# Reordering a filter's reversed copies in the SyncE queue, and moving the end of the last output slab from GpSimd to VectorE

One core of a Trainium2 chip. The metric is the device time of one execution in microseconds (us), median of several executions; "span" is the same from first to last instruction in the profiled execution.

## The reference

A layer norm, a spectral filter on one side, a gated feed-forward on the other, and a product:

```python
xn = _layernorm(x)                                    # x: 1 x 2048 x 640, bf16
s  = irfft2(rfft2(xn) * (w_r + 1j * w_i))             # filter w: 2048 x 321
g  = silu((gelu(xn @ w_gate) * (xn @ w_up)) @ w_down) # 640 -> 1536 -> 640
out = x + s * g
```

## The kernel before

The kernel is a list of tasks (instruction, engine, estimated cost, rank, predecessors), from which a planner in Python makes a fixed order for each engine ahead of time. It issues, at each step, the ready task with the lowest rank; a cost that is too low makes it believe that an engine (or the SyncE queue) is free early. The two Fourier transforms are matmuls and run interleaved with the feed-forward, so that TensorE is never out of work.

The filter is applied in eight groups G of rows. Each group needs its filter rows twice: as they are, and reversed. The reversal is done by DMA alone: a copy from DRAM to a DRAM scratch `D4` with a negative step (line 609, called "copy" below), and a load of the scratch into SBUF (line 632, "read-back"). Cut to that:

```python
for ri, w in enumerate((A_w_r, A_w_i)):
    for G in range(8):
        turned_w[G].append(add(lambda e, ...: nc.sync.dma_start(            # line 609: the reversing copy
            out=D4[:, b:8 * G + 8, ri, :], in_=bass.AP(..., ap=[[P * L, NSLAB], [-L, 8 * G + 8 - b], [1, LP]])),
            "SP", (430, 430), (2, G), after=[turned[3]] if G < 2 else [B_in[3]], ...))
...
def fetch(G):
    sw = Slot("W")                                     # three buffers WF in turn
    ...
    t = add(lambda e: go(e, 0, A_w_r), "SP", (430, 430), (3, G), after=hold, ...)   # line 625: rows as they are
    t = add(lambda e: go(e, 1, A_w_i), "SP", (430, 430), (3, G), after=hold, order=[t], ...)
    ...
    W_in[G] = add(back, "SP", (430, 430), (3, G), after=hold + turned_w[G], order=[t], ...)  # line 632: read-back
```

VectorE multiplies filter and spectrum (lines 738 and 746), forms `Y` (742, 749) and from it `R` (759, 761), which is what TensorE takes for the inverse transform (line 781, with the table TI as weights). TI is one more load in the same queue.

The last output slab (128 x 640) is finished in three parts of 256, 256 and 128 columns. The feed-forward's result lies in PSUM (`ps`), `th` is its tanh by ScalarE, `y` the filter's result, `sx` the input rows:

```python
def f1(e): (nc.gpsimd if last and lo == 0 else nc.vector).tensor_tensor(out=yg, in0=y, in1=G2, op=mult)   # line 954
def f2(e): (nc.gpsimd if last and lo == 0 else nc.vector).tensor_tensor(out=res, in0=yg, in1=sx, op=add)  # line 959
...
for lo, hi, tag in parts:
    ...
    a = add(tanh, "ACT", ...)                          # line 981
    if last and lo:                                    # parts 2 and 3
        t = add(early, "DVE", ...)                     # line 992: mc = y * ps    (f32)
        t = add(late, "DVE", ...)                      # line 995: yg = (th + 1) * mc
        t = add(... res = yg + sx ..., "DVE", ...)     # line 1001
        ... store part 2 by SyncE's queue, part 3 by ScalarE's (line 1004)
        continue
    done.append(add(silu, "DVE", ...))                 # line 986: G2 = (th + 1) * ps
    finish(lo, hi, ...)                                # lines 954, 959, store by SyncE's queue
```

Of the kernel before, what the change touches and what calls it, by code (L numbers as in the profile page):

```python
# [14 lines left out]
ALU = mybir.AluOpType  # L15
P = 128
S = 2048
D = 640
# [198 lines left out]
def c_dve(n, rate=2, psum=False, extra=0):  # L217
    d = ((120 if psum else 58) + n / rate) / 0.96 + extra
    return d + 10, d + 130
# [3 lines left out]
def kernel(  # L223
# [11 lines left out]
    nc = tc.nc  # L235
# [51 lines left out]
    add = plan.add  # L287
# [91 lines left out]
    t = add(blank, "DVE", (330, 400), (0, -9), new=[idle])  # L379
    t = warmed = keep_warm(6, [t])  # L380
# [225 lines left out]
    for ri, w in enumerate((A_w_r, A_w_i)):  # L606
        for G in range(8):
            b = 8 * G if G else 2
            turned_w[G].append(add(lambda e, ri=ri, w=w, G=G, b=b: nc.sync.dma_start(  # L609
                out=D4[:, b:8 * G + 8, ri, :], in_=bass.AP(tensor=w.tensor, offset=w.offset + (P - b) * L, ap=[[P * L, NSLAB], [-L, 8 * G + 8 - b], [1, LP]])),  # L610
                                   "SP", (430, 430), (2, G), after=[turned[3]] if G < 2 else [B_in[3]], size=82432, slow=1.7))
        for a, n, b, first, width in ((0, 8, 0, 1088, LP), (8, 7, 0, 1152, LP), (15, 1, 0, 1024, LP), (0, 15, 1, P - 1, LP), (15, 1, 1, S - 1, L)):
            turned_w[0].append(add(lambda e, ri=ri, w=w, a=a, n=n, b=b, first=first, width=width: nc.gpsimd.dma_start(
                out=D4[a:a + n, b, ri, 0:width], in_=rows(w, first, n, width)), "POOL", (600, 600), (9, ri, b, a), after=[roots[15]], size=5152))
        turned_w[0].append(add(lambda e, ri=ri, w=w: nc.gpsimd.dma_start(out=D4[15:16, 1, ri, L:LP], in_=w[0:1, 0:1]), "POOL", (600, 600),
                            (9, ri, 2), after=[roots[15]], size=64))

    def fetch(G):
        sw = Slot("W")
        W_slot[G] = sw  # L620

        def go(e, ri, w):
            sw.tile = WF[G % 3]
            c = 1 if G == 0 else 0
            nc.sync.dma_start(out=sw.tile[16 * c:P, 0, ri, 0:L], in_=w.rearrange("(k c) f -> c k f", c=P)[8 * G + c:8 * G + 8])

        def zero(e, ri, w):
            nc.sync.dma_start(out=sw.tile[0:16, 0, ri, 0:L],
                              in_=bass.AP(tensor=w.tensor, offset=w.offset, ap=[[64 * L, 2], [P * L, 8], [1, L]]))

        def back(e):
            nc.sync.dma_start(out=sw.tile[:, 1].rearrange("p r f -> p (r f)"), in_=D4[::-1, 8 * G:8 * G + 8].rearrange("a c r f -> c a (r f)"))
        hold = [stored[7]] + ([B_in[2 * G - 2]] if 0 < G < 3 else [])
        t = add(lambda e: go(e, 0, A_w_r), "SP", (430, 430), (3, G), after=hold, order=[W_in[G - 1]] if G else [], new=[sw], size=82176, slow=1.2)
        t = add(lambda e: go(e, 1, A_w_i), "SP", (430, 430), (3, G), after=hold, order=[t], use=[sw], size=82176, slow=1.2)
        if G == 0:
            for ri, w in enumerate((A_w_r, A_w_i)):
                t = add(lambda e, ri=ri, w=w: zero(e, ri, w), "SP", (430, 430), (3, G), after=hold, order=[t], use=[sw], size=10272, slow=1.2)
        W_in[G] = add(back, "SP", (430, 430), (3, G), after=hold + turned_w[G], order=[t], use=[sw], size=164352, slow=1.2)

    for G in range(8):
        fetch(G)
# [295 lines left out]
    def down(n1):  # L938
# [11 lines left out]
        def finish(lo, hi, done, rank, first):  # L950
            def f1(e):
                if first:
                    place(yg, (D,))
                (nc.gpsimd if last and lo == 0 else nc.vector).tensor_tensor(out=yg.tile[:, lo:hi], in0=y.tile[:, n1 % 2, lo:hi], in1=G2.tile[:, lo:hi], op=ALU.mult)

            def f2(e):
                if first:
                    place(res, (D,))
                (nc.gpsimd if last and lo == 0 else nc.vector).tensor_tensor(out=res.tile[:, lo:hi], in0=yg.tile[:, lo:hi], in1=sx.tile[:, lo:hi], op=ALU.add)  # L959
            slow = last and lo == 0  # L960
            t = add(f1, *(("POOL", (700, 800)) if slow else ("DVE", c_dve(hi - lo))), rank, after=[y_done[n1]] + done, new=[yg] if first else [], use=[y, G2] if first else [y, G2, yg])
            t = add(f2, *(("POOL", (700, 800)) if slow else ("DVE", c_dve(hi - lo))), rank, after=[t, xr], new=[res] if first else [], use=[yg, sx] if first else [yg, sx, res])
            dma(lambda: outv[:, n1, lo:hi], lambda: res.tile[:, lo:hi], (0, 0, n1), 256 * (hi - lo), after=[t], use=[res])

        for lo, hi, tag in parts:
            ps, th, mm = Slot(tag), Slot("th"), []
            for k in range(0, 12, 6):
                def go(e, k=k, lo=lo, hi=hi, ps=ps):
                    if k == 0:
                        place(ps, (512,))  # L970
                    for i in range(k, k + 6):
                        nc.tensor.matmul(ps.tile[:, 0:hi - lo], lhsT=uT[grp, ks[i]].tile[:, j * P:(j + 1) * P], rhs=Wd[:, ks[i], lo:hi],  # L972
                                         start=(i == 0), stop=(i == 11))
                step[0] += 1
                mm.append(add(go, "PE", c_pe(*[hi - lo] * 6), (1, step[0]), new=[] if k else [ps],
                              after=[u_done[grp, t] for t in ks[k:k + 6]] + mm + [d_in[t] for t in ks[k:k + 6]],
                              use=[uT[grp, t] for t in ks[k:k + 6]] + ([ps] if k else [])))

            def tanh(e, lo=lo, hi=hi, ps=ps, th=th):
                place(th, (320,), FP32)  # L980
                nc.scalar.activation(out=th.tile[:, 0:hi - lo], in_=ps.tile[:, 0:hi - lo], func=ACT.Tanh, scale=0.5)  # L981

            def silu(e, lo=lo, hi=hi, ps=ps, th=th):
                if lo == 0:
                    place(G2, (D,))
                nc.vector.scalar_tensor_tensor(out=G2.tile[:, lo:hi], in0=th.tile[:, 0:hi - lo], scalar=1.0, in1=ps.tile[:, 0:hi - lo],  # L986
                                               op0=ALU.add, op1=ALU.mult)
            yp = Slot("mc")

            def early(e, lo=lo, hi=hi, ps=ps, yp=yp):  # L990
                place(yp, (hi - lo,), FP32)
                nc.vector.tensor_tensor(out=yp.tile, in0=y.tile[:, n1 % 2, lo:hi], in1=ps.tile[:, 0:hi - lo], op=ALU.mult)

            def late(e, lo=lo, hi=hi, th=th, yp=yp):
                nc.vector.scalar_tensor_tensor(out=yg.tile[:, lo:hi], in0=th.tile[:, 0:hi - lo], scalar=1.0, in1=yp.tile,
                                               op0=ALU.add, op1=ALU.mult)
            a = add(tanh, "ACT", c_act(hi - lo), (0, step[0]), after=mm[-1:], new=[th], use=[ps])
            if last and lo:
                t = add(early, "DVE", c_dve(hi - lo, 1, True), (0, step[0]), after=mm[-1:] + [y_done[n1]], new=[yp], use=[ps, y])
                t = add(late, "DVE", c_dve(hi - lo, 1), (0, step[0]), after=[a, t] + done, use=[th, yp, yg])  # L1000
                t = add(lambda e, lo=lo, hi=hi: nc.vector.tensor_tensor(out=res.tile[:, lo:hi], in0=yg.tile[:, lo:hi], in1=sx.tile[:, lo:hi], op=ALU.add),
                        "DVE", c_dve(hi - lo), (0, step[0]), after=[t, xr], use=[yg, sx, res])
                if hi == D:
                    add(lambda e, lo=lo: nc.scalar.dma_start(out=outv[:, n1, lo:], in_=res.tile[:, lo:]), "ACT", (430, 430), (0, 0, n1),
                        after=[t], use=[res], size=256 * (hi - lo))
                else:
                    dma(lambda lo=lo, hi=hi: outv[:, n1, lo:hi], lambda lo=lo, hi=hi: res.tile[:, lo:hi], (0, 0, n1), 256 * (hi - lo), after=[t], use=[res])
                continue
            done.append(add(silu, "DVE", c_dve(hi - lo, 1, True), (0, step[0]), after=[a] + done, new=[] if lo else [G2],
                            use=[ps, th, G2] if lo else [ps, th]))  # L1010
            if last:
                finish(lo, hi, [done[-1]], (0, step[0]), lo == 0)
# [42 lines left out]
```

## Time and profile before

| | before |
|---|---|
| time, first three runs | 205.31 us (205.14 to 205.66) |
| profiled execution: time, span | 205.79 us, 204.0 us |
| TensorE busy | 195.1 us (96%) |
| last matmul ends; last store issued; span ends | 199.27; 201.03; 204.0 |

TensorE sets the pace: what matters is where it is *not* busy. The prediction shows the lines for it. One more line, from the timeline of SyncE's queue of the kernel before, tells how such lines are to be read (start, duration, engine, line, output and input):

```profile
85.17 0.63 SPq L632 DMA_DIRECT2D WF<-D  x1
```

The 0.63 us is the time that the queue spends on issuing. The Trainium skill, "Perfetto Trace Analysis", section "Per-instruction lifecycle: what the profiler-reported window actually captures", says that the window of such a DMA instruction holds the making of its descriptors and not the movement of data. This trace agrees: the same DMA landed 4.15 us after its issue, by the chain of waits.

### The profile page before, as it was taken

Reading aid. Unit: us, or ns where it says so; the run is one execution under the profiler, and the core shown is the slowest. Engines: PE = TensorE matmul, PEld = TensorE weight load, DVE = VectorE, ACT = ScalarE, POOL = GpSimd, SP = SyncE. Lnnn points to the kernel's source line nnn. Section 1 sums busy time; section 2 is a strip of 40 time slices with the busy share of each in tenths; the row PEclk is TensorE's granted clock in tenths of the full one; section 3 lists DMA queues with packets and bytes.
Section 4 is the critical chain, followed back from the end, with each engine's and each line's share of the span. In section 5 each row is a group of like instructions: output and inputs, shape, how many; then the busy total and the mean of one; then the engine's idle time right before and its main releaser. Section 6 shows DMA issues by size and latency. Waiting matters only on the chain.

```text
span 204.0 us, 4147 instructions
## 1 busy us (share of the span) xinstructions
PE 195.1 (96%) x1530; PEld 117.9 (58%) x1547; DVE 147.4 (72%) x312; ACT 129.1 (63%) x230; POOL 33.4 (16%) x72
## 2 busy tenths in 40 slices
PE   7999999999999999979999999999999999999990
PEld 2894444676444555756754555467765555557780
DVE  3589879999233259949999999943257789888763
ACT  4999699964822777666766776333467666675420
POOL 2413233799000000000000000000001122210211
PEclk9999999999999999999999999999999999999998
DMA  6999999698977957653243301116701243332421
GB/s 177 328 314 329 342 391 200 144 157 216 160 268 253 310 165 184 115 169 120 69 130 91 105 21 47 64 39 221 322 0 47 87 130 110 110 101 67 132 98 64
DMA packets 35894, 32.62 MB, mean 160 GB/s; under 512 B 10910, under 2 KB 32930, under 8 KB 35874
## 3 DMA queue, kind: packets, MB, share of 16 engines
q1 hardware_dynamic: 34434, 29.49, 49.5%
q0 software_dynamic: 1152, 2.66, 5.8%
q10 hardware_dynamic: 288, 0.20, 0.5%
q8 instruction: 12, 0.20, 0.4%
q14 instruction: 8, 0.07, 0.1%
HBM read 22.51 MB, written 9.19 MB: 155 GB/s over the span
## 4 chain that ended last, share of the span: by engine, by line
PE 74%; DMA 14%; SPq 4%; DVE 3%; issue 1%; ACT 1%; DVEq 0%
PE pu L894 20%; PE pg L894 19%; PE pu L972 11%; PE pg L972 11%; DMA BU<-D 5%; SPq L609 3%; DMA D<-mc 3%; PE sp L839 3%; DMA WF<-in_A_w_r_dram 2%; PE sp L815 2%; DMA WF<-D 2%; PE sp L781 2%; DMA X<-in_A_x_dram 2%; PE sp L541 2%; PE sp L706 1%
## 5 line engine op out<-in xcount | busy, mean ns | idle before, releaser
L894 PE MATMUL pu<-xnT,Wu 128*128 128x512 bf16 (+1 forms) x237 | 56.7, 365 | 0.5
L894 PE MATMUL pg<-xnT,Wg 128*128 128x512 bf16 (+1 forms) x236 | 56.3, 365 | 0.4
L911 DVE TENSOR_TENSOR uT<-pu,ge 128x512 bf16<-128x512 f32 x46 | 31.7, 689 | 21.2 <-PE pu L894 17.7
L972 PEld LDWEIGHTS <-uT 128*128 128x128 bf16 x396 | 37.9, 98 | 13.5
L907 ACT ACTIVATE ge<-pg 128x512 bf16<-128x512 f32 x46 | 27.5, 598 | 24.4 <-PE pg L894 23.5
L894 PEld LDWEIGHTS <-Wg 128*128 128x128 bf16 x285 | 25.1, 98 | 22.5 <-issue 0.3
L894 PEld LDWEIGHTS <-Wu 128*128 128x128 bf16 x285 | 25.0, 98 | 21.8
L935 POOL DMA_DIRECT2D xr<-in_A_x_dram x16 | 8.8, 550 | 135.8 <-DVE res L959 135.8
L972 PE MATMUL pg<-Wd,uT 128*128 128x320 bf16 (+2 forms) x204 | 30.7, 293 | 0.0
L297 ACT CAST ma<-sp 128x644 bf16<-128x644 f32 (+1 forms) x32 | 23.4, 793 | 9.7 <-PE sp L839 7.9
L972 PE MATMUL pu<-Wd,uT 128*128 128x320 bf16 (+1 forms) x192 | 29.5, 297 | 0.0
L297 ACT CAST IU<-sp 128x640 bf16<-128x640 f32 x16 | 10.9, 691 | 5.1 <-PE sp L781 5.1
L981 ACT ACTIVATE th<-pu 128x320 f32<-128x320 f32 (+1 forms) x16 | 7.0, 435 | 10.7 <-PE pu L972 10.1
L981 ACT ACTIVATE th<-pg 128x320 f32<-128x320 f32 (+2 forms) x17 | 7.3, 429 | 10.0 <-PE pg L972 8.5
L297 ACT CAST Vt<-sp 128x640 bf16<-128x640 f32 x16 | 10.8, 691 | 3.7 <-PE sp L815 3.7
L986 DVE SCALAR_TENSOR_TENSOR G<-th,pg 128x320 bf16<-128x320 f32 (+1 forms) x16 | 7.7, 479 | 6.9 <-ACT th L981 6.9
L297 ACT CAST mc<-sp 128x640 bf16<-128x640 f32 x16 | 10.7, 704 | 1.3 <-PE sp L542 1.3
L986 DVE SCALAR_TENSOR_TENSOR G<-th,pu 128x320 bf16<-128x320 f32 x15 | 7.3, 484 | 5.3 <-ACT th L981 5.1
L434 POOL TENSOR_TENSOR RSTD<-MVA,mh 128x1 f32<-128x1 f32 x12 | 8.9, 743 | 6.6 <-DVE MVA L416 5.9
L419 ACT ACTIVATE th<-X 128x640 bf16<-128x640 bf16 x11 | 8.1, 739 | 1.7 <-DMA D<-th 1.6
L857 DVE TENSOR_TENSOR mb<-ma 128x640 bf16<-128x640 bf16 x8 | 3.9, 493 | 7.0 <-ACT ma L297 7.0
L738 DVE TENSOR_TENSOR mc<-WF,mb 128x1288 bf16<-128x1288 bf16 x8 | 6.6, 826 | 3.1 <-DMA WF<-D 3.0
(110 smaller groups left out, 248.5 us busy)
## 6 DMA issues: line engine op xcount, KB each, us to landing
BU<-D SPq DMA_DIRECT2D x8, 640.0 KB
D<-mc SPq DMA_DIRECT2D x8, 320.0 KB
xr<-in_A_x_dram POOLq DMA_DIRECT2D x16, 160.0 KB, 2.6
D<-IU SPq DMA_DIRECT2D x8, 320.0 KB
out_dram<-res SPq DMA_DIRECT2D x15, 160.0 KB
Wg<-in_B_w_gate_dram SPq DMA_DIRECT2D x6, 320.0 KB
Wu<-in_B_w_up_dram SPq DMA_DIRECT2D x6, 320.0 KB
Wd<-in_B_w_down_dram SPq DMA_DIRECT2D x6, 320.0 KB
```

What stands on the lines that cost most here:

```text
L297: return nc.scalar.copy(out=out, in_=in_) if e == "ACT" else nc.vector.tensor_copy(out=out, in_=in_)
L419: nc.scalar.activation(out=place(junk, (D,)), in_=x, func=ACT.Copy, scale=-1.0 / D, accum_out=less)
L434: nc.gpsimd.tensor_tensor(out=rstd, in0=var, in1=mh, op=ALU.pow)
L609: turned_w[G].append(add(lambda e, ri=ri, w=w, G=G, b=b: nc.sync.dma_start(out=D4[:, b:8 * G + 8, ri, :], in_=bass.AP(tensor=w.tensor, off ...
L738: nc.vector.tensor_tensor(out=sM.tile, in0=sw.tile, in1=sV.tile, op=ALU.mult)
L894: nc.tensor.matmul(ps.tile[:, lo:hi], lhsT=w[:, c, t * P:(t + 1) * P], rhs=XR[:, c, lo:hi] if early else xnT[:, c, grp * 512 + lo:grp * 51 ...
L907: nc.scalar.activation(out=ge.tile, in_=pg.tile if src is None else src, func=ACT.Gelu_apprx_tanh)
L911: nc.vector.tensor_tensor(out=u.tile, in0=pu.tile if src is None else src, in1=ge.tile, op=ALU.mult)
L935: nc.gpsimd.dma_start(out=sx.tile, in_=xv[:, n1, :])
L972: nc.tensor.matmul(ps.tile[:, 0:hi - lo], lhsT=uT[grp, ks[i]].tile[:, j * P:(j + 1) * P], rhs=Wd[:, ks[i], lo:hi], start=(i == 0), stop=(i ...
L981: nc.scalar.activation(out=th.tile[:, 0:hi - lo], in_=ps.tile[:, 0:hi - lo], func=ACT.Tanh, scale=0.5)
L986: nc.vector.scalar_tensor_tensor(out=G2.tile[:, lo:hi], in0=th.tile[:, 0:hi - lo], scalar=1.0, in1=ps.tile[:, 0:hi - lo], op0=ALU.add, op1 ...
```

## The change

Intent: a reversing copy of group G should be issued just ahead of the loads of the group in front of it, instead of all copies together ahead of group 2's read-back; the planner's cost of an issue is put nearer to the trace's 0.64 us; and GpSimd is taken off the end, its part and the middle part both going through lines 986, 954 and 959 on VectorE.

```diff
-   "SP", (430, 430), (2, G), after=[turned[3]] if G < 2 else [B_in[3]], ...            # copies, line 609
+   "SP", (650, 650), (2, G) if G < 2 else (3, G - 1.5), after=[turned[3]] if G < 2 else [B_in[3]], ...
 ...
-   t = add(lambda e: go(e, 0, A_w_r), "SP", (430, 430), (3, G), ...                    # loads and read-back
+   t = add(lambda e: go(e, 0, A_w_r), "SP", (680, 680), (3, G), ...                    # (all four lines alike)
 ...
-   (nc.gpsimd if last and lo == 0 else nc.vector).tensor_tensor(out=yg..., op=ALU.mult)
+   (nc.gpsimd if n1 in () else nc.vector).tensor_tensor(out=yg..., op=ALU.mult)        # never GpSimd; f2 alike
 ...
-   if last and lo:
+   if last and hi == D:                                                                # only part 3 by 992, 995
```

More of the change, by code (lines that the diff above doesn't have):

```diff
@@ L610 @@
                 out=D4[:, b:8 * G + 8, ri, :], in_=bass.AP(tensor=w.tensor, offset=w.offset + (P - b) * L, ap=[[P * L, NSLAB], [-L, 8 * G + 8 - b], [1, LP]])),
-                                   "SP", (430, 430), (2, G), after=[turned[3]] if G < 2 else [B_in[3]], size=82432, slow=1.7))
+                                   "SP", (650, 650), (2, G) if G < 2 else (3, G - 1.5), after=[turned[3]] if G < 2 else [B_in[3]], size=82432, slow=1.7))
         for a, n, b, first, width in ((0, 8, 0, 1088, LP), (8, 7, 0, 1152, LP), (15, 1, 0, 1024, LP), (0, 15, 1, P - 1, LP), (15, 1, 1, S - 1, L)):
@@ L633, in fetch @@
         hold = [stored[7]] + ([B_in[2 * G - 2]] if 0 < G < 3 else [])
-        t = add(lambda e: go(e, 0, A_w_r), "SP", (430, 430), (3, G), after=hold, order=[W_in[G - 1]] if G else [], new=[sw], size=82176, slow=1.2)
-        t = add(lambda e: go(e, 1, A_w_i), "SP", (430, 430), (3, G), after=hold, order=[t], use=[sw], size=82176, slow=1.2)
+        t = add(lambda e: go(e, 0, A_w_r), "SP", (680, 680), (3, G), after=hold, order=[W_in[G - 1]] if G else [], new=[sw], size=82176, slow=1.2)
+        t = add(lambda e: go(e, 1, A_w_i), "SP", (680, 680), (3, G), after=hold, order=[t], use=[sw], size=82176, slow=1.2)
         if G == 0:
             for ri, w in enumerate((A_w_r, A_w_i)):
-                t = add(lambda e, ri=ri, w=w: zero(e, ri, w), "SP", (430, 430), (3, G), after=hold, order=[t], use=[sw], size=10272, slow=1.2)
-        W_in[G] = add(back, "SP", (430, 430), (3, G), after=hold + turned_w[G], order=[t], use=[sw], size=164352, slow=1.2)
+                t = add(lambda e, ri=ri, w=w: zero(e, ri, w), "SP", (680, 680), (3, G), after=hold, order=[t], use=[sw], size=10272, slow=1.2)
+        W_in[G] = add(back, "SP", (680, 680), (3, G), after=hold + turned_w[G], order=[t], use=[sw], size=164352, slow=1.2)
     for G in range(8):
@@ L953, in f1 @@
                     place(yg, (D,))
-                (nc.gpsimd if last and lo == 0 else nc.vector).tensor_tensor(out=yg.tile[:, lo:hi], in0=y.tile[:, n1 % 2, lo:hi], in1=G2.tile[:, lo:hi], op=ALU.mult)
+                (nc.gpsimd if n1 in () else nc.vector).tensor_tensor(out=yg.tile[:, lo:hi], in0=y.tile[:, n1 % 2, lo:hi], in1=G2.tile[:, lo:hi], op=ALU.mult)
             def f2(e):
@@ L958, in f2 @@
                     place(res, (D,))
-                (nc.gpsimd if last and lo == 0 else nc.vector).tensor_tensor(out=res.tile[:, lo:hi], in0=yg.tile[:, lo:hi], in1=sx.tile[:, lo:hi], op=ALU.add)
-            slow = last and lo == 0
-            t = add(f1, *(("POOL", (700, 800)) if slow else ("DVE", c_dve(hi - lo))), rank, after=[y_done[n1]] + done, new=[yg] if first else [], use=[y, G2] if first else [y, G2, yg])
-            t = add(f2, *(("POOL", (700, 800)) if slow else ("DVE", c_dve(hi - lo))), rank, after=[t, xr], new=[res] if first else [], use=[yg, sx] if first else [yg, sx, res])
+                (nc.gpsimd if n1 in () else nc.vector).tensor_tensor(out=res.tile[:, lo:hi], in0=yg.tile[:, lo:hi], in1=sx.tile[:, lo:hi], op=ALU.add)
+            slow = n1 in ()
+            t = add(f1, *(("POOL", (2000, 2100)) if slow else ("DVE", c_dve(hi - lo))), rank, after=[y_done[n1]] + done, new=[yg] if first else [], use=[y, G2] if first else [y, G2, yg])
+            t = add(f2, *(("POOL", (2000, 2100)) if slow else ("DVE", c_dve(hi - lo))), rank, after=[t, xr], new=[res] if first else [], use=[yg, sx] if first else [yg, sx, res])
             dma(lambda: outv[:, n1, lo:hi], lambda: res.tile[:, lo:hi], (0, 0, n1), 256 * (hi - lo), after=[t], use=[res])
```

## The prediction

> **What bounds the kernel now.** I read the page's busy shares first, then the waits, then the timeline around the longest wait of TensorE, then the chain at the end.
>
> ```profile
> PE 195.1 (96%) x1530; PEld 117.9 (58%) x1547; DVE 147.4 (72%) x312; ACT 129.1 (63%) x230; POOL 33.4 (16%) x72
> ```
>
> TensorE (PE) is busy for 195.1 of 204.0 us. A change that leaves its instructions alone can win only out of the other 8.9 us. Set against each other, the instruction streams of the two kernels hold the same TensorE and ScalarE rows in the same order; only the order of the SyncE queue, the last rows of VectorE and two rows of GpSimd differ. So I ask where the 8.9 us are. TensorE's first matmul starts at 1.21 and its last ends at 199.27, so about 5.9 us lie at the two ends. The waits inside:
>
> ```profile
> PE sp L781 <- DVE R L759: 1.4, 1, 1.4
> ...
> PE sp L781 <- DVE R L761: 0.3, 1, 0.3
> ```
> ```profile
> DVE mc L738 <- DMA WF<-D: 3.0, 1, 3.0
> ```
>
> There is one real stall after the start-up: TensorE waits for R, which VectorE (DVE) makes, and VectorE itself once waits 3.0 us for a load of the filter (WF<-D, the reversed half of a group, read back from a DRAM scratch). The chain of waits joins the two:
>
> ```profile
> 84.52 0.60 SPq L609
> ...
> 85.17 4.15 DMA WF<-D
> ...
> 89.44 0.83 DVE mc L738
> ```
>
> Line 609 is the reversing copy, DRAM to DRAM. In the queue's timeline twelve such copies (groups 2 to 7, real and imaginary) are issued back to back from 76.66 to 85.12, about 0.64 us each, and only then comes the read-back of group 2 (line 632), which needs just the two of its own group, issued at 76.66 and 77.35. It lands 4.15 us later; VectorE had finished its earlier work at about 86.4 and sat idle until 89.44. The R that TensorE waits for belongs to group 1, but stands behind group 2's product (line 738) in VectorE's order.
>
> ```profile
> 89.65 0.98 PE L972 MATMUL pu<-Wd,uT 128*128 128x320 bf16 x6
> 92.03 0.47 PE L781 MATMUL sp<-R,TI 128*128 128x256 bf16 x4 [1.40 <-DVE R L759]
> 92.33 0.98 PE L972 MATMUL pu<-Wd,uT 128*128 128x320 bf16 x6
> 93.57 0.48 PE L781 MATMUL sp<-R,TI 128*128 128x256 bf16 x4 [0.26 <-DVE R L761]
> 93.89 0.97 PE L972 MATMUL pg<-Wd,uT 128*128 128x320 bf16 x6
> ```
>
> The first column is the start. Ends of matmuls are modelled and overlap the next start, so I count from start to start. Unhindered, six 320-wide matmuls take 0.81 us (84.35 to 85.16) and the four of line 781 take 0.30 (92.03 to 92.33). From 89.65 to 93.89 there are 4.24 us for work of 0.81 + 0.30 + 0.81 + 0.31 = 2.23 us. The loss is **2.0 us**; the waits' own 1.40 + 0.26 = 1.66 is the lower reading of it.
>
> The end of the kernel, by the timeline:
>
> ```profile
> 198.64 0.39 ACT L981 ACTIVATE th<-pu 128x256 f32<-128x256 f32 x1 [0.93 <-PE pu L972]
> 199.06 0.42 DVE L992 TENSOR_TENSOR mc<-s,pu 128x256 f32<-128x256 bf16 x1 [0.70 <-ACT th L981]
> 199.19 0.67 POOL L959 TENSOR_TENSOR res<-yg,xr 128x256 bf16<-128x256 bf16 x1
> 199.51 0.62 DVE L995 SCALAR_TENSOR_TENSOR yg<-th,mc 128x256 bf16<-128x256 f32 x1
> 200.06 0.28 DVE L992 TENSOR_TENSOR mc<-s,pg 128x128 f32<-128x128 bf16 x1
> 200.26 0.28 DVE L1001 TENSOR_TENSOR res<-yg,xr 128x256 bf16<-128x256 bf16 x1
> 200.77 0.22 DVE L1001 TENSOR_TENSOR res<-yg,xr 128x128 bf16<-128x128 bf16 x1
> 201.03 0.36 ACTq L1004 DMA_DIRECT2D out_dram<-res  x1
> ```
>
> The 256-wide product of line 995 takes 0.62 us while GpSimd works beside it; the 128-wide one takes 0.28. At 0.96 elements per ns, 128 elements more should cost 0.13, so some 0.41 would do.
>
> **What the Trainium skill says.** "DMA: Bandwidth & Descriptors", section "Anatomy of one DMA", says that a semaphore wait of a DMA happens on the issuing sequencer, before dispatch, not in the DMA engines. The trace agrees: one queue instruction follows another, and line 632 goes out 0.05 us after the twelfth copy. Its place in the queue is what the change buys. The same section puts most of a DMA's fixed cost, about 2 us, into the write receipt; here issue to landing is 4.15 us for 161 KB behind copies, and I use the 4.15. "SBUF — State Buffer", section "Who interferes with whom", says that a VectorE instruction with two SBUF inputs contends with a GpSimd instruction that reads SBUF, and that one is blocked. The 0.62 us beside GpSimd's 0.67 fit this; the trace does not prove it.
>
> **The change, part by part.**
>
> *Queue order.* Nothing is added or removed; the same copies and loads are issued. In the changed order, after group 1's read-back (72.69, whose wait for the regrouped data I leave as it is), come: one filter load of group 2, four copies (groups 2 and 3), the other filter load, the TI table, and the read-back of group 2. By the durations of before that is 73.3 + 0.65 + 4 x 0.64 + 0.65 + 0.5 = 77.7. The read-back must also wait until group 2's second copy has landed: issued at about 74.6, and with 4.15 us assumed for it (my choice; no view of before gives a copy's landing) that is 78.8. Landing another 4.15 us later: about 83. VectorE asks at 86.4. So the 2.96 us of idle vanish whole, with 3 us in hand.
>
> What does TensorE get of that? With line 738 at 86.4 the rest follows: 0.74 and 0.40 for lines 738 and 749, then line 986, whose input th ends at 87.74, then the two R instructions, done at about 89.1. TensorE wants that R at 90.46 (89.65 + 0.81). The second R would be done at about 90.6; TensorE wants it at 91.57. Neither stalls. VectorE gains 2.96, TensorE its full 2.0, the difference being slack. All later work of TensorE, VectorE and ScalarE hangs on each other and moves up by 2.0: -2.0 us.
>
> *Tail.* GpSimd's two instructions (0.66 + 0.67) go to VectorE at about 0.2 us each from start to start (200.06 to 200.26 for a 128-wide, 200.26 to 200.46 for a 256-wide one). They fill the 0.70 us that VectorE idles from 198.36 to 199.06: 198.39 and 198.70, done at 198.98. In the old time scale the rest is then: line 986 on the middle 256 columns from 199.06 to 199.47 (it waits for the same th, so nothing is won there); line 992 on the last 128 from 199.62 (its th ends at 199.59) to 199.90; line 954 (256) from 199.82 to 200.10; line 995 (128) from 200.02 to 200.30; line 959 (256) at 200.22; line 1001 (128) from 200.42 to 200.64. The last store leaves at about 200.68 instead of 201.03: -0.35 us. The middle store leaves at 200.54, and the one that GpSimd's result held last in SyncE's queue leaves early. The gain comes from replacing line 995's 0.62 on the critical stretch by a 256-wide line 954 that runs alone.
>
> Sum: 205.31 - 2.0 - 0.35 = 202.96. I say **203.0 us**, 1.1% less.
>
> **The rivals.** (1) *The stall moves to another load.* TI is issued at 77.2 instead of 73.3; TensorE first needs it at 83.6. With 4.7 us to landing (the chain's figure for the filter load right behind TI) that is 81.9: 1.7 us in hand. If it came late, up to 1 us would be lost: 204. The read-back of group 3 now stands behind five copies of later groups: issue about 83 to 87, landing by 91, wanted at about 94.3 (96.30 less 2.0). Groups 4 and later have as much room. (2) *The copy-to-read-back wait is long.* If a copy takes 8 us to land, group 2's read-back lands near 87 and blocks the queue too; then a part of the 2 us comes back, 203.5 to 204. Against it: all DMA engines together are busy only 0.5 to 0.8 here. (3) *VectorE takes the place of the load.* It is nearly solidly busy from 89.44 to 111, and an order with less idle might still be late somewhere; but TensorE shows no wait for VectorE in that stretch, and VectorE moves up by at least as much as TensorE. (4) *The tail wins nothing*: line 959 for the first part needs the result buffer of slab 13, stored from 195.8; if that lands after 198.7, VectorE is held up in the last 3 us. With about 0.3 us of idle behind it a small delay is absorbed; otherwise 203.3.
>
> **Range and chances.** Counting the stall by waits (1.66) and no tail gain gives 203.65; 2.1 and 0.5 give 202.7. The runs of before spread over 0.5 us. I take 202.3 to 203.9. Over 2% faster would be below 201.2, which the 8.9 us hardly hold: 0.02. Slower by 2% would need a new stall of some 6 us: 0.01. Within 2%: 0.97.
>
> **What would show it.** Right: no VectorE wait for WF<-D in the middle; line 781's waits gone; TensorE's work after 94 earlier by 2.0; last store 0.35 us closer to TensorE's end (1.76 us now, 201.03 less 199.27). Wrong: a TensorE wait on TI's load, a wait of the queue at line 632, or a VectorE wait at a later group's line 738.

## The result, and the profile after

| | before | after |
|---|---|---|
| time, five runs each of the same rounds | 205.66 us (205.14 to 205.80) | 202.99 us (202.89 to 203.14) |
| span of the profiled execution | 204.0 | 201.2 |
| TensorE busy | 195.1 | 195.1 |
| VectorE's wait for WF<-D | 2.96 | none |
| last matmul ends | 199.27 | 197.26 |
| last store issued | 201.03 | 198.67 |
| from that to SyncE's first drain, to the end | 1.99, 2.96 | 1.69, 2.52 |

The ratio is 0.9876 (95% interval 0.986 to 0.9892). It is computed as the mean time of one kernel's fast runs over that of the other's of the same rounds, so it is not quite the ratio of the medians quoted. At the 2% threshold this counts as "same"; the difference is clear of noise all the same.

The page's busy shares of the kernel after: the same TensorE work in a shorter span.

```profile
PE 195.1 (97%) x1530; PEld 118.2 (59%) x1547; DVE 147.7 (73%) x314; ACT 128.9 (64%) x230; POOL 32.1 (16%) x70
```

The waits of TensorE, kernel after; this is the only one listed, and it is the start-up:

```profile
PE sp L369 <- DVE uT L362: 1.2, 1, 1.2
```

The timeline of SyncE's queue after (start, duration): a copy of group 2, then TI and, right behind it, group 2's read-back, 7 us earlier than the 85.17 of before, and group 3's read-back.

```profile
74.40 0.63 SPq L609 DMA_DIRECT2D D<-in_A_w_r_dram  x1
...
77.67 0.46 SPq L304 DMA_DIRECT2D TI<-tab_ti  x1
78.24 0.63 SPq L632 DMA_DIRECT2D WF<-D  x1
...
85.63 0.75 SPq L632 DMA_DIRECT2D WF<-D  x1
```

VectorE's timeline after: line 738 starts with no wait in brackets; the second pair of R instructions ends at 90.21 + 0.49 = 90.70.

```profile
86.38 0.82 DVE L738 TENSOR_TENSOR mc<-WF,mb 128x1288 bf16<-128x1288 bf16 x1
...
90.21 0.49 DVE L761 TENSOR_TENSOR R<-Y 64x644 bf16<-64x644 bf16 x1
```

TensorE's timeline after, the stretch that took 4.24 us before (89.65 to 93.89): from 89.65 to 91.87 it is 2.22 us now, with no gap.

```profile
89.65 0.98 PE L972 MATMUL pu<-Wd,uT 128*128 128x320 bf16 x6
90.46 0.46 PE L781 MATMUL sp<-R,TI 128*128 128x256 bf16 x4
...
91.57 0.47 PE L781 MATMUL sp<-R,TI 128*128 128x256 bf16 x4
91.87 0.97 PE L972 MATMUL pg<-Wd,uT 128*128 128x320 bf16 x6
```

From there on each matmul starts 2.01 or 2.02 us earlier than before, to the last one. The tail after:

```profile
197.04 0.42 DVE L986 SCALAR_TENSOR_TENSOR G<-th,pu 128x256 bf16<-128x256 f32 x1
...
197.60 0.29 DVE L992 TENSOR_TENSOR mc<-s,pg 128x128 f32<-128x128 bf16 x1
...
198.42 0.22 DVE L1001 TENSOR_TENSOR res<-yg,xr 128x128 bf16<-128x128 bf16 x1
198.67 0.35 ACTq L1004 DMA_DIRECT2D out_dram<-res  x1
```

The last store leaves 1.41 us after TensorE's end (198.67 less 197.26), against 1.76. So of the 2.8 us by which the profiled span fell, 2.01 lie ahead of TensorE's end, 0.35 between that and the last store's issue, and 0.44 behind the last store's issue. The third I had not put in the sum. The line that shows it is the one for the drains at the end of the program (durations in ns, then first and last start in us), of the kernel before and after:

```profile
L1050 SPq DRAIN  x3: 7/13/114, 203.0 to 203.7; - x3
```
```profile
L1050 SPq DRAIN  x3: 7/11/13, 200.4 to 200.9; - x3
```

SyncE gets to its first drain when the stores have landed (its list of waits names them there, 1.0 us before and 0.8 us after). The view rounds these starts to a tenth; the kept trace has 203.02 and 200.35, that is 1.99 us after the last store's issue before and 1.69 us after it. The rest (0.97 and 0.83 us) is the closing of the program. So the 0.44 us are 0.31 of quicker landing and 0.14 of shorter closing. Times from an issue to a drain are taken from the kept traces in this way below.

### The profile page after: what moved, and what is told of

The parts are those of the page before. It is cut to its first block, busy times and chain, and to the rows that moved or that the text cites. A ratio compares the mean times of both kernels' runs of the same rounds, so it can differ in the third digit from the quotient of the medians.

```text
span 201.2 us, 4145 instructions
## 1 busy us (share of the span) xinstructions
PE 195.1 (97%) x1530; PEld 118.2 (59%) x1547; DVE 147.7 (73%) x314; ACT 128.9 (64%) x230; POOL 32.1 (16%) x70
## 3 DMA queue, kind: packets, MB, share of 16 engines
q0 software_dynamic: 1152, 2.66, 6.1%
## 4 chain that ended last, share of the span: by engine, by line
PE 94%; DMA 2%; ACT 1%; issue 1%; DVE 1%; SPq 0%; DVEq 0%
PE pu L894 26%; PE pg L894 25%; PE pg L972 13%; PE pu L972 13%; PE sp L706 3%; PE sp L839 3%; PE sp L781 2%; PE sp L815 2%; DMA X<-in_A_x_dram 2%; PE sp L541 2%; PE sp L679 2%; PE sp L699 1%; PE sp L833 1%; PE sp L487 1%; PE sp L542 0%
## 5 line engine op out<-in xcount | busy, mean ns | idle before, releaser
L986 DVE SCALAR_TENSOR_TENSOR G<-th,pu 128x320 bf16<-128x320 f32 (+1 forms) x16 | 7.7, 480 | 5.4 <-ACT th L981 5.1
L759 DVE TENSOR_TENSOR R<-Y 64x644 bf16<-64x644 bf16 x16 | 7.8, 490 | 0.4
```

The lines of the kernel that those rows point to most:

```text
L759: nc.vector.tensor_tensor(out=o, in0=Yf[:, ::-3, :], in1=Yf[:, 1:3, :], op=ALU.subtract)
L986: nc.vector.scalar_tensor_tensor(out=G2.tile[:, lo:hi], in0=th.tile[:, 0:hi - lo], scalar=1.0, in1=ps.tile[:, 0:hi - lo], op0=ALU.add, op1 ...
```

## The experiments

Twelve kernels in three calls, each call on one chip with its own runs of the kernel before. All twelve gave the right result. Two warnings about the times. Two executions of the kernel before (208.41 and 207.64 us) count as slow, being over 1.5% above the fastest of the same kernel, and are left out. The other times of the kernel before scattered over 2 us on these chips (204.4 to 206.9 in the first call), so differences between kernels of one call, and traces, weigh more than the ratios to it. And in two profiles the regrouped data BU<-D came late and cost 1.6 or 1.7 us far ahead of the changed places; these are the lines of it for the kernel q_only, from TensorE's waits and from the queue's timeline:

```profile
PE sp L679 <- DMA BU<-D: 1.6, 1, 1.6
```
```profile
62.91 3.29 SPq L586 DMA_DIRECT2D BU<-D  x4
```

The four loads already left late: the queue had waited 7.0 us for the store ahead of them (D<-mc) in both profiles, 5.5 to 6.2 in the twelve others, and their issues took 3.29 and 3.39 us together instead of 2.25 to 2.5. It hit the profiled execution of q_only and tail_a_full (205.84 and 205.16 us) and, by the times, not their five others; such a profile is read from the end of TensorE's work, not by its span.

### First call: the parts alone

**q_only**: only the first two hunks of the diff (ranks and costs). **t_only**: only the tail's hunks. **tail_a_full**: the whole change, but

```diff
-            if last and hi == D:
+            if last and lo:
```

**tail_b_full**: the whole change, but

```diff
-            (nc.gpsimd if n1 in () else nc.vector)
+            (nc.gpsimd if last and lo == 0 else nc.vector)     # in f1 and f2
```

> The queue part alone (new ranks and costs of copies and loads; the tail as before). Theory A (the read-back of group 2 went out too late, TensorE lost 2.0 us): VectorE's 3.0 us wait for WF<-D and both waits of line 781 are gone, TensorE's last matmul ends 2.0 us earlier (197.26), the stretch from there to the end stays as before (4.7 us), time -2.0 +-0.2 against before. Rival (the queue order bought more than that, for instance earlier stores of IU or less DMA traffic at the end): -2.5 or more, and the tail part alone then gives nothing.

> The tail part alone, the queue as before. Theory A (only the shorter VectorE chain counts): the last store leaves 1.4 us after TensorE's last matmul instead of 1.76, time -0.35. Theory B (the three last stores, 160 KB within 0.85 us, also get in each other's way, and the first part's store now leaves 3.5 us earlier): the stretch from the last store's issue to the end of the span shrinks from 2.97 to about 2.5 us as well, time -0.7 to -0.9. Rival: nothing, the measured 2.7 us were all the queue's.

> The changed kernel, but the middle 256 columns keep the old path (line 992 and line 995); GpSimd's two instructions are on VectorE. Theory A: VectorE's two extra instructions fall behind th, on the chain (line 992 still waits for th, so the idle 0.7 us is not used); the last store leaves some 0.1 to 0.2 us LATER than with GpSimd (about 1.9 us after TensorE's last matmul), time 0.1 to 0.2 above the queue part alone. Rival (GpSimd's slowness and its blocking of VectorE was the cost): 0.2 below the queue part alone.

> The changed kernel, but the first 256 columns stay on GpSimd; only the middle part goes the new path (line 986, 954, 959). Theory A: the last store leaves about 1.4 us after TensorE's last matmul, as in the changed kernel (line 954 of the middle part touches GpSimd's line 959 by less than 0.1 us), so time 0.3 below the queue part alone and within 0.1 of the changed kernel. Rival (GpSimd blocks VectorE whenever it runs): 0.2 to 0.3 slower than the changed kernel.

| kernel | time (median, 6 runs) | range | last store after line 986 of part 1 | issue of last store to first drain |
|---|---|---|---|---|
| before (10 fast of 11 runs) | 205.53 | 204.36 to 206.90 | 3.08 | 1.99 |
| q_only | 203.86 | 203.49 to 205.84 | 3.08 | 1.99 |
| t_only | 204.49 | 204.21 to 206.92 | 2.73 | 1.68 |
| tail_a_full | 203.42 | 203.19 to 205.16 | 3.28 | 1.58 |
| tail_b_full | 203.06 | 202.91 to 203.46 | 2.74 | 1.70 |

The last two columns are differences of starts in each kernel's own trace. (Line 986 of part 1 starts at 197.95 before, at 195.93 after; the changed kernel has 2.74 and 1.69.)

The queue part alone takes away the wait for WF<-D and the waits of line 781, as expected, and leaves the tail as it was. By time it is 1.7 below the median of before in this call. Between the two kernels with the new tail path the queue part is worth less: 204.49 less 203.06 is 1.4 (tail_b_full also leaves part 1 on GpSimd). The tail part alone is 1.0 below before by the medians, but its ratio to before is not clear of noise (0.9919 to 1.0021). With the new queue it is worth 203.86 less 203.06, 0.8 us (0.65 by the means, without q_only's profiled execution), so the rival that the queue did it all falls. This is near theory B's 0.7 to 0.9 and not the 0.35 of my sum. In t_only's trace the last store leaves 1.41 us after TensorE's end, as both theories had it, and from there to the end of the span it is 2.66 us, between the 2.97 of before and the 2.5 of theory B.

The tail's own split is the more instructive. Timeline of tail_a_full, where GpSimd's work is on VectorE but part 2 keeps the old path:

```profile
199.35 0.42 DVE L995 SCALAR_TENSOR_TENSOR yg<-th,mc 128x256 bf16<-128x256 f32 x1
...
200.98 0.35 ACTq L1004 DMA_DIRECT2D out_dram<-res  x1
```

Line 995 takes 0.42 us here, without GpSimd beside it, and 0.62 with it in both traces of before: the 0.2 us go with GpSimd's work, and 0.42 is near the 0.41 of the prediction. Yet the last store leaves 0.2 us *later* than with GpSimd (3.28 against 3.08), because the two extra instructions now stand behind part 2's line 992, which waits for `th`. And still the time is 0.44 below q_only. The expectation was 0.1 to 0.2 above it, so it failed in the time, though not in the chain. By the trace the longer chain and a quicker landing (1.58 against 1.99, the store of part 1 now leaving ahead of that of part 2) make 0.2 less; the rest is not explained. Timeline of tail_b_full, where GpSimd keeps its part:

```profile
197.28 0.67 POOL L959 TENSOR_TENSOR res<-yg,xr 128x256 bf16<-128x256 bf16 x1
...
197.91 0.29 DVE L954 TENSOR_TENSOR yg<-s,G 128x256 bf16<-128x256 bf16 x1
```

With part 2 on the new path GpSimd is done (197.95) when VectorE's first product with two SBUF inputs comes up (197.91), and the chain is as short as in the changed kernel (2.74). So it is the new path of part 2 that shortens the chain; taking GpSimd off adds nothing to it. In both kernels part 1's store also leaves ahead of part 2's, which leads to the next call.

### Second call: how late is too late, and the last stores

**after_again**: the changed kernel as it is. **ahead12**: in the changed kernel, whatever the planner says, the eight copies of groups 4 to 7 are emitted ahead of group 2's read-back (their own places then emit nothing):

```diff
         def back(e):
+            if G == 2: [copies[g, r]() for g in range(4, 8) for r in (0, 1)]   # each copy is sent once
             nc.sync.dma_start(out=sw.tile[:, 1]..., in_=D4[...])
```

**ahead12_tabs**: the same, with the three small tables (i1, im, it) sent ahead of it too. **store_last**: in the changed kernel, the store of part 1 is held until that of part 2 has been issued:

```diff
-            dma(lambda: outv[:, n1, lo:hi], lambda: res.tile[:, lo:hi], ...)
+            add(lambda e: held.append((lo, hi)) if last and lo == 0 else
+                [nc.sync.dma_start(out=outv[:, n1, a:b], in_=res.tile[:, a:b]) for a, b in [(lo, hi)] + held], "SP", ...)
```

> The changed kernel again, unchanged, as the measure for the other three runs of this call (kernels on different chips differed by up to 0.5 us, and single executions by 2 us where the regrouped data BU<-D landed late). Theory A: 203.0 +-0.2, no wait for WF<-D, PE's own wait list holds nothing but the start-up, unless the profiled execution has the late BU<-D of two earlier profiles (then 1.7 us more in that one execution).

> The changed kernel, but the eight copies of groups 4 to 7 go out ahead of group 2's read-back (12 copies ahead of it, as in the kernel before; TI stays ahead of them, the three small tables behind). The read-back leaves at about 83.4 instead of 78.2 and lands at about 87.5; VectorE asks at 86.4. Theory A (VectorE's wait reaches TensorE only beyond a slack of 1.3 us: R is ready at 89.15, wanted at 90.46): VectorE waits 1.1 us for WF<-D, TensorE 0 to 0.1, time within 0.15 of the changed kernel. Rival 1 (each us that VectorE waits costs TensorE the same): +1.1. Rival 2 (it is the mere number of copies ahead, by DMA load, that hurt): +2.0 as in the kernel before.

> As the former, with the three small tables ahead of the read-back too, as in the kernel before: 1.45 us later, it leaves at about 84.9 and lands at about 89.0. Theory A: VectorE waits 2.6 us, TensorE 1.1 at the first R and 0.4 at the second, time +1.6 (1.3 to 1.9) above the changed kernel. Rival 1: +2.6. Rival 2: the same as the former.

> The changed kernel, but the store of the first 256 columns is held back behind that of the middle ones, as in the kernel before (all the computing as in the changed kernel). Theory B (three stores within a us delay the last landing): last store leaves at the same time after TensorE's end (1.4 us), but 1.95 instead of 1.73 us pass from its issue to the first drain of SyncE, time +0.2 to +0.3. Rival (the shorter landing had other grounds, for instance GpSimd's idleness or chance): within 0.1 of the changed kernel.

| kernel | time (median, 6 runs) | range |
|---|---|---|
| before (11 runs) | 205.14 | 204.37 to 206.39 |
| after_again | 203.24 | 203.03 to 203.40 |
| ahead12 | 203.31 | 203.08 to 203.88 |
| ahead12_tabs | 204.70 | 204.23 to 205.43 |
| store_last | 203.56 | 203.37 to 204.18 |

after_again, at 203.24, is just outside its expected 203.0 +-0.2. ahead12 has all twelve copies ahead of the read-back, as the kernel before, and loses 0.07 us by the medians. Rival 2, the mere number of copies, is out. Lines of VectorE's and TensorE's timelines, ahead12:

```profile
87.86 0.83 DVE L738 TENSOR_TENSOR mc<-WF,mb 128x1288 bf16<-128x1288 bf16 x1 [1.46 <-DMA WF<-D]
...
91.99 0.48 PE L781 MATMUL sp<-R,TI 128*128 128x256 bf16 x4 [0.26 <-DVE R L761]
```

and of ahead12_tabs:

```profile
89.72 0.83 DVE L738 TENSOR_TENSOR mc<-WF,mb 128x1288 bf16<-128x1288 bf16 x1 [3.14 <-DMA WF<-D]
...
92.31 0.47 PE L781 MATMUL sp<-R,TI 128*128 128x256 bf16 x4 [1.57 <-DVE R L759]
```

The read-back left at 83.51 and 85.56 (expected 83.4 and 84.9), and in ahead12 VectorE could start 4.35 us after that, not 4.1; so both profiled waits are longer than expected (1.1 and 2.6). Putting the three tables ahead, with all other orders alike, brings 1.4 us of the loss back: what counts is when the read-back leaves. Times: +0.07 and +1.46, as theory A expected; rival 1 would have had +1.1 and +2.6. One figure of theory A failed: it took 1.3 us of slack, from the first R alone. In ahead12's profiled execution (203.55) VectorE waits 1.46 us and TensorE already loses 0.52, at the second R: that one runs out of slack first (table of the third call).

store_last gets slower by 0.32, and its trace says where. ScalarE's store of part 3, SyncE's of part 1, and the first drain:

```profile
198.85 0.35 ACTq L1004 DMA_DIRECT2D out_dram<-res  x1
```
```profile
199.09 0.42 SPq L963 DMA_DIRECT2D out_dram<-res  x1
```
```profile
L1050 SPq DRAIN  x3: 7/13/114, 200.8 to 201.5; - x3
```

From part 3's store to the drain 1.97 us pass, against 1.69 in both traces of the changed kernel, with the computing unchanged; the closing after it takes 0.97 us, against 0.83 and 0.82. So the order of the stores counts, and its size is as theory B expected. The ground of theory B, that stores within a us get in each other's way, is not shown by this run: held back, the store of part 1 leaves 0.24 us behind part 3's, and from there the drain comes after 1.73 us, nearly as in the changed kernel. What is lost is lost by leaving later.

In the kernel before it is not so simple: there the store of part 1 leaves 0.04 us ahead of part 3's, and still 1.99 us pass. Sorted by the distance between the last two issues, the other thirteen traces give 1.99 to 2.01 us at 0.04 (before, before_again, q_only), 1.68 to 1.70 at 0.14 (eight traces) and 1.56 to 1.58 at 0.47 and 0.56 (tail_c, tail_a_full). This fits stores that hinder each other when they leave close together; but which part they carry and what left before them changes along with the distance, and no run takes these apart. The prediction named the store of part 1 and gave it no price.

### Third call: the scatter, the planner's costs, the rival TI, and a better tail

**before_again**: the kernel before. **rank_full**: the changed kernel with the planner's old costs, `(430, 430)` instead of `(650, 650)` and `(680, 680)`; it then puts eleven copies and the three tables ahead of group 2's read-back. **ti_late**: the changed kernel with TI sent behind the three tables and two more copies. **tail_c**: the changed kernel with a forced order on VectorE in the tail:

```diff
-  t = add(early, "DVE", ..., after=mm[-1:] + [y_done[n1]], ...)
+  t = add(early, "DVE", ..., after=mm[-1:] + [y_done[n1]], order=[line 954 of part 2], ...)
-  t = add(late, "DVE", ..., after=[a, t] + done, ...)
+  t = add(late, "DVE", ..., after=[a, t] + done, order=[line 959 of part 2], ...)
```

> The kernel before, unchanged, for a second trace. Its times scatter over 2 us (204.4 to 206.4 on one chip), those of the changed kernel over 0.4. From the runs so far: TensorE's loss = VectorE's wait for WF<-D less 1.0 us (0.15 of idle that the wait swallows, 0.87 of slack of the second R). Theory A: what scatters is that wait, since the chain from the regrouped data through the twelve copies to the read-back is all DMA; a run near 205 us (span near 203.2) has a wait of about 2.3 us and a loss of 1.3, so that the queue part is worth 1.3 there and the tail part 0.7. Rival: the wait is 3.0 again whatever the time of the run, and the scatter has other grounds.

> The changed kernel with the new ranks of the copies, but the planner's old cost of 430 ns for copies and filter loads (the trace has 640). The planner then places eleven copies and the three tables ahead of group 2's read-back: it should leave at about 84.5 and land at about 88.7. Theory A: VectorE waits 2.3 us, TensorE loses 1.3, time 1.3 (+-0.3) above the changed kernel (that is about 204.5). Rival (the rank is the change, the costs are cosmetic): within 0.2 of the changed kernel.

> The changed kernel, but TI goes out behind the three small tables and two more copies, at about 81.1 instead of 77.7; the read-back of group 2 half a us earlier. Measures my first rival, how near TI was to being late: TensorE first wants it at 83.5. Theory (about 4 us to landing, as the read-back): TensorE waits 1.6 us for TI's load at 83.5, time +1.6 (1.0 to 2.0). Rival (it lands within 2.5 us): no wait, time within 0.2.

> An attempt at a better version: in the changed kernel's tail, the middle part's line 954 is put into VectorE's idle 0.14 us ahead of the last part's line 992, and its line 959 ahead of line 995, so that the middle store leaves 0.3 us earlier and is out of the way of the last one. Theory A/B: last store leaves within 0.05 us of the changed kernel's time, landing 0.1 us sooner, time -0.05 to -0.15. Rival: no difference, the landing of the last store has a floor of 1.7 us.

| kernel | time (median) | range |
|---|---|---|
| before (10 fast of 11 runs) | 205.34 | 204.43 to 206.76 |
| before_again (6) | 205.22 | 204.21 to 206.28 |
| rank_full (6) | 204.07 | 202.98 to 204.31 |
| ti_late (4) | 205.17 | 204.63 to 207.14 |
| tail_c (6) | 202.85 | 202.79 to 202.89 |

before_again's wait, from VectorE's timeline:

```profile
89.11 0.83 DVE L738 TENSOR_TENSOR mc<-WF,mb 128x1288 bf16<-128x1288 bf16 x1 [2.52 <-DMA WF<-D]
```

It is 2.5 us in an execution of 205.48, 3.0 in the one of 205.79 that I predicted from. The wait does differ from execution to execution, as theory A says. Of the 0.44 us between the waits, 0.26 are one copy, whose issue held the queue for 1.35 us in the one execution and 1.09 in the other (about 0.6 is usual); why it varies is open. TensorE lost 0.45 us less, the time fell by 0.31 only, and no profile caught the kernel before near 204.4; so that the wait makes all of the scatter is not shown.

rank_full is 0.8 to 1.1 us slower than the changed kernel (203.24 and 202.99 on other chips; expected 1.3), and 1.2 slower than tail_c of the same call, which differs from the changed kernel in the tail's order alone. The costs are not cosmetic: with the new rank and the old costs the planner takes issues to be cheap and pushes nearly all copies ahead again. Its wait, in a profiled execution that was fast for it (203.63):

```profile
87.92 0.83 DVE L738 TENSOR_TENSOR mc<-WF,mb 128x1288 bf16<-128x1288 bf16 x1 [1.31 <-issue]
```

Here the releaser is named "issue", the profile having found none; by its place in the order and its input it is the same read-back, issued at 84.06. This is less than expected: 84.5 for the read-back, 2.3 for VectorE's wait and 1.3 for TensorE's loss, which is 0.34 in this execution (next table). The reverse, the new costs with the old rank, was not run.

These traces, taken together, give the rule that the whole change rests on. TensorE's loss is counted from start to start over the stretch of the prediction, less the 2.23 us of work in it:

| trace | read-back leaves | VectorE waits | TensorE loses | difference |
|---|---|---|---|---|
| after | 78.24 | 0 | 0 | |
| rank_full | 84.06 | 1.31 | 92.37 - 89.80 - 2.23 = 0.34 | 0.97 |
| ahead12 | 83.51 | 1.46 | 92.31 - 89.56 - 2.23 = 0.52 | 0.94 |
| before_again | 84.94 | 2.52 | 93.55 - 89.76 - 2.23 = 1.56 | 0.96 |
| before | 85.17 | 2.96 | 93.89 - 89.65 - 2.23 = 2.01 | 0.95 |
| ahead12_tabs | 85.56 | 3.14 | 94.17 - 89.76 - 2.23 = 2.18 | 0.96 |

About the first 0.96 us of VectorE's wait are free, and every us beyond costs a us. (t_only's trace is left out: TensorE's granted clock dropped in that very stretch, and six 320-wide matmuls took 1.52 us in the view instead of 0.98.) The slack fits the trace of after: the second R is ready at 90.70 and wanted at 91.57, which is 0.87, and VectorE has 0.16 us of idle ahead of line 986 that a wait swallows, less some hundredths for the handing over.

ti_late, TensorE's timeline:

```profile
85.54 0.47 PE L781 MATMUL sp<-R,TI 128*128 128x256 bf16 x4 [1.74 <-DMA TI<-tab_ti]
```

TI left at 80.95 and TensorE could start 4.59 us later. In the changed kernel, where it leaves at 77.67, it is there by about 82.3 by the same figure, an estimate, and is wanted at 83.6: 1.3 us to spare. The span of its profile is 203.1, 1.6 above after_again's 201.5; by the medians it is 1.9, across two chips.

tail_c is the fastest of all in its runs, and the most even. Its last store and first drain:

```profile
198.72 0.35 ACTq L1004 DMA_DIRECT2D out_dram<-res  x1
```
```profile
L1050 SPq DRAIN  x3: 7/11/13, 200.3 to 200.9; - x3
```

1.56 us from issue to drain instead of 1.69; the chain on VectorE is no shorter (2.75 from line 986 of part 1). It did not run in one call with the changed kernel, whose medians on two chips were 202.99 and 203.24, so that it is faster by a tenth or so is likely by the trace and not proven by the times. Against before its ratio is 0.987 (0.9838 to 0.9902).

## Why the prediction was right

The time was 202.99, predicted 203.0 (202.3 to 203.9). By its steps:

- **The bound and the stall.** TensorE sets the pace and lost 2.0 us at one place, waiting for R behind VectorE's wait for a read-back that stood behind twelve copies. Shown: its last matmul moved by 2.01 us; ahead12_tabs, built from the changed kernel, brings the stall back by sending the eight later copies and the three tables ahead of the read-back. The copies alone bring back little (ahead12, 0.07 us by the medians): what counts is when the read-back leaves.
- **The queue's new times.** Read-back at 77.7 to 78.8, found 78.24. The 4.15 us assumed for a copy's landing were too many: group 2's second copy went out at 75.07 and had landed when the read-back left, at most 3.2 us later. R ready at about 89.1 and 90.6, found 89.15 and 90.70. Group 3's read-back between 83 and 87, found 85.63. VectorE asked for it at 93.48 and not at 94.3, since it had moved by 2.8 us and not by 2.0; it still found it there, and no later group waits.
- **VectorE's gain is not TensorE's.** The prediction had 2.96 against 2.0, "the difference being slack". The five traces with a wait put the slack at 0.96.
- **The tail's chain, -0.35.** Found 0.35 (1.76 to 1.41). The prediction gave as its ground line 954 in place of line 995's 0.62, "that runs alone". The first half is right; running alone is not needed (tail_b_full), and GpSimd's removal by itself lengthens the chain (tail_a_full).
- **The mis-sized term is the tail**: -0.35 in the sum, 0.66 by the traces, 0.65 to 0.8 by the times of q_only and tail_b_full. What it missed is 0.31 us between the last store's issue and the first drain. They go with the order and spacing of the last three stores (store_last gives 0.28 of them back, but by a store that leaves later still); how a store holds the other up is not shown.
- **The closing, 0.14, was missed too**, and by the traces it is not the tail's. It goes with a last drain of SyncE of 113 to 118 ns in place of 7 to 12. The closing takes 0.97 or 0.98 us in all six traces with eleven or twelve copies ahead of group 2's read-back, the new tail (t_only) as well as the old, and 0.82 or 0.83 in seven of the other eight, q_only with the old tail among them; the eighth is store_last, with 0.97. Why is open.
- **Why the sum fits all the same.** That it fits to 0.01 is luck. The sum starts from 205.31, the median of three runs; the five runs of the same rounds have 205.66, so the change measured is 2.67 us, and 2.35 was predicted. The queue's 2.0 was read from one execution (205.79) above the median; in another (205.48) TensorE lost 1.56, and by times the queue part is worth 1.4 (t_only against tail_b_full) to 1.7 (before against q_only). The tail gave more than its share, the queue at times less. The range would have held either.
- **The rivals.** TI stayed 1.3 us clear (predicted 1.7), and would have cost the time if sent 3 us later. The wait for the copies did not block the queue: the read-back left 0.11 us after TI's issue ended. The result buffer did not hold line 959 back.

## What to carry to other kernels

When a wait of a side engine is taken away, price it at the bound engine, by start-to-start times: here the first 0.96 us of a 3 us wait were free. A DMA's place in its issuing queue is a cost, here about 0.64 us per copy and 0.48 per table in front of it, and a planner that takes a copy for 0.43 puts the urgent load behind nearly all of them (rank_full). At the very end, order the stores so that only the smallest is left when the last result is done: here the other order cost 0.3 us (store_last).

## What the Trainium skill lacked or had wrong

- "DMA: Bandwidth & Descriptors", section "Anatomy of one DMA", gives about 50 ns for dispatch and "small, variable" for descriptor generation, both for DMAs issued by GpSimd. Each copy here (about 128 rows of 644 bytes) held SyncE's queue for 0.55 to 0.71 us, and in nearly every trace one held it for 0.74 to 1.66. For that queue the page has a count of sequencer cycles per DMA instruction of earlier generations, without a clock, and no time for the issue of a many-row DMA.
- The same section's fit, about 2.0 us plus bytes over 436 GB/s (made for another issuing path), would give an estimated 2.4 us for the 161 KB read-back. From issue to landing it took 4.15 us in the chain of waits of before, with other transfers under way; the TI table of 512 KB was there after 4.59 us, where the fit gives an estimated 3.2.
- "SBUF — State Buffer", section "Who interferes with whom", is borne out: line 995, with two SBUF inputs, took 0.62 us beside GpSimd and 0.42 without, while line 986, whose second input lies in PSUM, took 0.41 to 0.42 beside GpSimd or not. The page speaks of the loser blocking for the other's whole instruction; here the loss was 0.2 us of a 0.67 us instruction of which 0.35 us were still to run when line 995 came up (the profile's spans on GpSimd are rough).
- No page says how the stores of the last us set the end of a program: 1.56 to 2.01 us from part 3's store to the first drain, by the order and spacing of the stores, and then 0.82 to 0.98 us of closing, by something that stays open.
- No page gives a time for an issue that takes longer in single executions: the four loads BU<-D held the queue for 3.29 and 3.39 us in two profiles and for 2.25 to 2.5 in the twelve others. The store ahead of them was late in the same two (7.0 us of waiting against 5.5 to 6.2); the cause stays open.
